# Seven-product second MoE: narrowing steps spread anew, second pass with 512 tokens first, products stored from ACT's queue

## The chip, the core and the metric

The kernel runs on one core of a Trainium2 chip. The metric is the device time of one execution in microseconds (us); three runs of the kernel before give its median.

## What is computed

A talking-heads attention over 1792 tokens feeds a first MoE layer (SoLU with a layer norm), which feeds a second one (squared ReLU). The result is the second layer's output, 1792 x 768, in float32.

```python
def _moe_ref(x, w_in, w_out, g_ln):          # d_model 768, d_ff 1024
    h = x @ w_in
    e = np.exp(h - np.max(h, axis=-1, keepdims=True))
    solu = h * (e / (np.sum(e, axis=-1, keepdims=True) + 1e-09))
    ...
    return (ln @ w_out).astype(np.float32)    # ln: solu normalised over d_ff, times g_ln

def _moe2_ref(x, w_in, w_out):                # d_model 768, d_ff 2048
    r = np.maximum(x @ w_in, 0.0)
    return (r * r @ w_out).astype(np.float32)

def reference(...):
    x = attention(q, k, v, w_pre, w_post)     # 1792 tokens x 768
    x = _moe_ref(x, **moe)
    return _moe2_ref(x, **moe2)
```

## The kernel before

**Split numbers.** TensorE multiplies in fp32r. Each float32 operand is split into a high part (a cast, on ACT) and a low part (a subtraction, on DVE or POOL), and each product is the sum of three matmuls.

**Three stages.** Attention takes the first 466 us and is not touched. The first MoE goes in tiles of 128 tokens, m = 0 to 13, until about 720 us. The second MoE takes the rest.

**First MoE, one tile.** PE computes `h1(m)`, 36 matmuls of 128 x 512. DVE then runs the norm, `norm1(m)`, from the maximum at L652 to the scaling at L668. PE transposes the previous tile (`zt`, L685; copied by ACT at L687 and DVE at L688). Every three tiles the output products `out1` become due, 24 matmuls each into a bank called ps_o; from m = 4 two of them run per tile, 20 in the loop. ACT copies each from ps_o into a tile o (L707, two buffers), and its DMA to x2D (L708) is issued by SP. Ten further products run behind the loop.

**Narrowing.** The second MoE's weights lie in memory as 64-bit floats. Beside the first MoE and the start of the second, 64 pieces of 128 x 384 are brought to float32. For each piece ACT computes a square wsq (L75, one buffer), and DVE runs four steps: L76, L80, L84 and L88; L88 needs wsq. Then SP stores the piece to w2D and loads the piece after next into the raw tile wr (two buffers). `filler()` is a call that runs one DVE step; the program places such calls by hand. In the loop there are 5 behind the norm of each tile from m = 4 and 4 behind each of its two `out1`, 13 per tile; the ten products behind the loop have three each. `need(n)` runs all steps that are missing when a load needs a piece.

**Second MoE.** d_ff is worked through in 8 steps of 256, twice: pass 0 for tokens 0 to 1023, pass 1 for tokens 1024 to 1791. `GRP` cuts each pass into two token groups, q = 0 and q = 1. A step is (it, q), it = 0 to 15. In a step PE first computes `h2` of the **next** step (L930, 36 matmuls of as many columns as the group has tokens), then `y2` of this step: seven products (a Strassen-like scheme), each of one to two blocks of three matmuls with 384 columns (L999), into one of three buffers ps_y. Each product is added to its own y on DVE (L1029). In it 0 there is nothing to add to, so y is a copy, from DVE (L1031) and ACT (L1033) by turns. The last it of each pass (7 and 15) is plain: seven sums on DVE (`join`, L992), then four products of twice the length and adds at L1017, each followed by a store.

Around it ACT computes relu and square (L938, L939) and the high parts of g, of the weights `ti` and `to` (L964, L834, L914). POOL computes the four sums s of the seven-product scheme (L953) and most low parts (L968, L838, L915). In the odd steps (q = 1) DVE computes two low parts of the next `ti` (L838), two of g (L968), four differences tT of the next `to` (L907, `sum_to`) and, in the second pass, two low parts of `to` (L915), all ahead of the step's adds; then come the narrowing steps. The tokens' tile x2 is loaded from x2D and split by `load_x2` and `split_x2` (L807 on ACT, L808).

**What sets the order.** The order on each engine is the order in which the program is written; engines wait for each other by semaphores. `hook(k)` is called behind product k and places the next step's splits of g there. Nothing reorders.

Of the kernel before, what the change touches and what calls it, by code (L numbers as in the profile page):

```python
# [18 lines left out]
def kernel(  # L19
# [16 lines left out]
    nc = tc.nc  # L36
    B, D, _ = qT.shape
# [8 lines left out]
    CC = DM // 128  # L46
# [7 lines left out]
    x2D = dram.tile([DM, NT], F32, name="x2D")  # L54
# [3 lines left out]
    NE = F2 // FE  # L58
# [67 lines left out]
    for b in range(B):  # L126
        for (i0, n) in CHUNKS:
            c, nb, oa = len(chunks), -(-n // R), 0
# [288 lines left out]
    def h1(m):  # L417
        t = xs.pop(m)
        pool = psi_p if m % 2 else psh_p
        ps = pool.tile([128, 2, 512], F32, tag="h", name="ps_h")  # L420
        for cc in range(CC):
            for (a, w) in ((0, 0), (0, 1), (1, 0)):
                for u in range(2):
                    nc.tensor.matmul(  # L424
                        out=ps[:, u],
                        lhsT=t[:, a, cc],
                        rhs=w1i[cc][:, w, u * 512:(u + 1) * 512],
                        start=(cc == 0 and a == 0 and w == 0),
                        stop=(cc == CC - 1 and a == 1),
                    )  # L430
            yield True
        hps[m] = ps

    def run(part):
        for _ in part:
            pass
# [184 lines left out]
    def load_w1_out(kk):  # L621
        r = m1_p.tile([128, DM], F32, tag="raw", name="w1oraw", bufs=3)
        nc.sync.dma_start(out=r, in_=w1oD[kk * 128:(kk + 1) * 128, :])
        return r
# [7 lines left out]
    def load_x(m):  # L632
        r = m1_p.tile([128, CC, 128], F32, tag="raw", name="xraw", bufs=3)
        nc.sync.dma_start(
            out=r, in_=xD[:, m * 128:(m + 1) * 128].rearrange("(c p) t -> p c t", p=128)
        )
        return r

    def split_x(m, r):
        t = m1_p.tile([128, 2, CC, 128], F32R, tag="xs", name="xs", bufs=2)  # L640
        nc.scalar.copy(t[:, 0], r)
        nc.gpsimd.tensor_tensor(out=t[:, 1], in0=r, in1=t[:, 0].bitcast(F32), op=ALU.subtract)
        xs[m] = t
# [48 lines left out]
    def out1(grp, cc):  # L692
        zT = zts[grp]
        t0 = grp * GT * 128
        width = min(GT * 128, NT - t0)
        ps = ps1_p.tile([128, 512], F32, tag="o", name="ps_o", bufs=2)
        for k in range(K1):
            for i, (w, a) in enumerate(((0, 0), (0, 1), (1, 0))):
                nc.tensor.matmul(  # L699
                    out=ps[:, 0:width],  # L700
                    lhsT=w1o[k][:, w, cc * 128:(cc + 1) * 128],
                    rhs=zT[:, a, k, 0:width],
                    start=(k == 0 and i == 0),
                    stop=(k == K1 - 1 and i == 2),
                )
        o = m1_p.tile([128, GT * 128], F32, tag="o", name="o1", bufs=2)
        nc.scalar.copy(o[:, 0:width], ps[:, 0:width])  # L707
        nc.sync.dma_start(out=x2D[cc * 128:(cc + 1) * 128, t0:t0 + width], in_=o[:, 0:width])  # L708

    w2raw = {}  # L710
    stored = [0]
# [34 lines left out]
    for m in range(NTILE):  # L746
        if m + 2 < NTILE:
            xr[m + 2] = load_x(m + 2)
        if m:
            run(h1(m))  # L750
        norm = norm1(m)
        next(norm)
        if m > 0:
            zt(m - 1)
        run(norm)
        if m + 2 < NTILE:
            split_x(m + 2, xr.pop(m + 2))
        for kk in range(len(w1o), min(K1, len(w1o) + 2)):
            wr[kk] = load_w1_out(kk)
        for kk in sorted(wr):  # L760
            split_w1_out(kk, wr.pop(kk))
        for _ in range(5 if m > GT else 0):
            filler()
        if m > GT and (m - 1) % GT == 0:
            outs += [((m - 1) // GT - 1, cc) for cc in range(CC)]
        for _ in range(2):
            if outs:
                out1(*outs.pop(0))
                for _ in range(4):
                    filler()  # L770


# [5 lines left out]
    wi2 = tc.tile_pool(name="wi2", bufs=1, side="left", reuse_waits="tile")  # L778
    wi2_p = wi2.__enter__()
    TG = 512  # L780
    GRP = [[(0, 512), (512, 512)], [(1024, 256), (1280, 512)]]
    NI = 2 * NE
    x2 = {}
    x2r = []
# [1 line left out]
    def load_x2(p, q, c):  # L786

        t0, n = GRP[p][q]
        k = TG // n
        r = wi2_p.tile([128, TG], F32, tag="x2r", name="x2r", bufs=3)  # L790
        nc.sync.dma_start(
            out=r.rearrange("p (k t) -> p k t", k=k),
            in_=x2D[c * 128:(c + k) * 128, t0:t0 + n].rearrange("(k p) t -> p k t", p=128),
        )
        x2r.append(r.rearrange("p (k t) -> p k t", k=k))

    def split_x2(p, q, c, eng):
        n = GRP[p][q][1]
        k = TG // n
        if c % 2 == 0:  # L800
            pool = wi2_p if q == 0 or c == 0 else m2_p
            t = pool.tile([128, 2, 2, TG], F32R, tag=f"x2_{q}_{c // 2}", name="x2")
            x2.setdefault((p, q), []).append(t)
        t = x2[p, q][-1]
        hi, lo = [t[:, a, c % 2:c % 2 + k, 0:n] for a in range(2)]
        r = x2r.pop(0)
        nc.scalar.copy(hi, r)  # L807
        eng.tensor_tensor(out=lo, in0=r, in1=hi.bitcast(F32), op=ALU.subtract)  # L808
# [101 lines left out]
    def split_to(it, k0, k1):  # L910
        for k in range(k0, min(k1, len(bsrc[it]))):
            r = bsrc[it][k]
            t = m2_p.tile([128, 2, HM], F32R, tag="to", name="to", bufs=9)
            nc.scalar.copy(t[:, 0], r)  # L914
            (nc.vector if it >= NE and k < 2 else nc.gpsimd).tensor_tensor(  # L915
                out=t[:, 1], in0=r, in1=t[:, 0].bitcast(F32), op=ALU.subtract
            )
            to.setdefault(it, []).append(t)
# [4 lines left out]
    def h2(it, q):  # L923
        n = GRP[it // NE][q][1]
        rs = []
# [32 lines left out]
    def hi_g(it, q):  # L958
        g = gs.setdefault((it, q), [])
        k = len(g)  # L960
        if k < len(gsrc[it, q]):
            w = GRP[it // NE][q][1] // 2
            g.append(m2_p.tile([128, 2, TG // 2], F32R, tag="g", name="g", bufs=9)[:, :, 0:w])
# [8 lines left out]
    def store_y(p, q, i, u, t):  # L972
        t0, n = GRP[p][q]
        w = n // 2
# [4 lines left out]
    def join(p, q):  # L979

        na = GRP[p][q][1] // 256
        p1, p2, p6, p7, p5, p4, p3 = [t[:, 0:na] for t in ys.pop((p, q))]
# [60 lines left out]
    for c in range(2, CC):  # L1043
        split_x2(0, 1, c, nc.vector)
        if c + 3 < CC:
            load_x2(0, 1, c + 3)
    sum_to(0)
    split_to(0, 0, 2)
    for j in range(4):
        load_ti(1, j)  # L1050
# [5 lines left out]
    for i, (it, q) in enumerate(steps):  # L1056
        p, e = divmod(it, NE)
        more = i + 1 < len(steps)
        nxt = it + 1 < NI

        if q and nxt:
            for j in (2, 3):
                ti_lo(it + 1, j, nc.vector)
        for k in range(2):
            lo_g(it, q, k, nc.vector)
        if q == 0:
            split_to(it, 2, 7)
            if nxt:
                for j in range(2):
                    ti_hi(it + 1, j)  # L1070
                    ti_lo(it + 1, j, nc.gpsimd)
        elif nxt:
            sum_to(it + 1)
            split_to(it + 1, 0, 2)
        if e == NE - 2 and q == 1:
            join(p, 0)
        if e == NE - 1 and q == 0:
            join(p, 1)
        if p == 0 and e == NE - 1:
            if q == 0:  # L1080
                for c in range(0, CC, 2):
                    split_x2(1, 0, c, nc.vector)
                    load_x2(1, 1, c // 2)
            else:
                for c in range(3):
                    split_x2(1, 1, c, nc.vector)
                    load_x2(1, 1, c + 3)
        for _ in range((5 if q else 11) + (4 if it == 0 else 0)):
            filler()
        if more:  # L1090
            h2(*steps[i + 1])

        if q == 0:
            if nxt:
                for j in (2, 3):
                    ti_hi(it + 1, j)
                load_to(it + 1, B[3])
        elif it + 2 < NI:
            for j in range(4):
                load_ti(it + 2, j)  # L1100
        if it == NE - 2 and q == 1:
            for c in range(0, CC, 2):
                load_x2(1, 0, c)

        def hook(k):
            if more:
                g = gs[steps[i + 1]]
                hi_g(*steps[i + 1])
                if len(g) > k + 2:
                    lo_g(*steps[i + 1], k + 2, nc.gpsimd)  # L1110
            if it == NE - 1 and q == 1 and k < 3:
                split_x2(1, 1, k + 3, nc.gpsimd)

        y2(it, q, hook)
        if q and it + 2 < NI:
            for fu in B[:3]:
                load_to(it + 2, fu)
# [58 lines left out]
```

## Time and profile before

| | us |
|---|---|
| median of three runs | 1237.52 |
| lowest and highest run | 1234.03, 1239.85 |
| the profiled execution | 1237.23 |
| its span in the trace | 1235.5 |
| PE busy | 1167.3 (94%) |
| DVE busy | 899.6 (73%) |
| ACT busy | 594.8 (48%) |
| POOL busy | 527.3 (43%) |
| first MoE's tiles with narrowing (DVE, L652 of m = 4 to L652 of m = 13) | 502.33 to 668.06 |

A timeline row holds the start, the time until the last of its instructions ended, the engine, the line, the operation, the tiles (written <- read), and how many instructions were put together; a bracket gives the idle time before it and what ended that. A matmul's end is modelled, and a busy PE may be slower than it could be, so the length of rows of like work is to be compared too.

### The profile page before, as it was taken

The numbers are of one execution on the slowest core, as the hardware profiler recorded it, in microseconds if no ns is written. First come the engines' busy times: TensorE is split into PE (matmuls) and PEld (weight loads), VectorE is DVE, ScalarE is ACT, GpSimd is POOL, SyncE is SP. The second block draws the span as 40 slices with busy tenths as digits, with TensorE's granted clock in tenths as the row PEclk, the third lists the DMA queues.
The fourth block names the chain that finished last, engine by engine and source line by source line (L and its number), as shares of the span: only waits on it lengthen the run. The fifth ranks groups of instructions, "written<-read, shape, count | busy, mean of one in ns | idle before, by whom it ended". The sixth has DMA issues, their size and how long they took to land. (4 is left out here: it accounts for less than half of the span.)

```text
span 1235.5 us, 22011 instructions
## 1 busy us (share of the span) xinstructions
PE 1167.3 (94%) x7599; PEld 975.5 (79%) x7599; DVE 899.6 (73%) x1612; ACT 594.8 (48%) x1485; POOL 527.3 (43%) x696
## 2 busy tenths in 40 slices
PE   9999999999999999999997995899999999999888
PEld 4777777777777778899986974788888898888777
DVE  4777777767776666777677567798888784777775
ACT  4565655666666544423322344643454446554441
POOL 2342233223222435311010356666657638777760
PEclk9999999999999999999999897999899999999999
DMA  6874765576574442544544763433342243212202
GB/s 175 214 208 161 215 196 182 184 212 194 159 218 144 147 147 91 156 126 143 166 131 121 239 201 92 145 128 110 102 129 64 77 148 110 71 58 62 65 10 77
DMA packets 131690, 172.19 MB, mean 139 GB/s; under 512 B 24443, under 2 KB 114171, under 8 KB 131579
## 3 DMA queue, kind: packets, MB, share of 16 engines
q1 hardware_dynamic: 130795, 170.51, 45.4%
q8 instruction: 61, 1.00, 0.3%
q14 instruction: 50, 0.41, 0.1%
q10 hardware_dynamic: 784, 0.27, 0.1%
HBM read 96.82 MB, written 35.39 MB: 107 GB/s over the span
## 5 line engine op out<-in xcount | busy, mean ns | idle before, releaser
L999 PE MATMUL ps_y<-to,g 128*128 128x384 f32 x1197 | 233.1, 352 | 45.3 <-DVE y L1029 26.9
L999 PEld LDWEIGHTS ps_y<-to,g 128*128 128x128 f32 x1197 | 221.3, 199 | 54.2 <-ACT r L938 24.6
L930 PE MATMUL ps_h<-x,ti 128*128 128x512 f32 (+1 forms) x1152 | 240.7, 366 | 1.7 <-ACT x L807 1.1
L930 PEld LDWEIGHTS ps_h<-x,ti 128*128 128x128 f32 x1152 | 197.7, 189 | 38.3 <-DVE x L808 2.0
L293 PEld LDWEIGHTS ps_post<-w,e 120*112 120x112 f32 (+1 forms) x1440 | 168.3, 177 | 67.5 <-issue 48.3
L307 DVE COPY at<-ps_post 112x480 f32<-112x480 f32 x180 | 117.1, 651 | 108.6 <-PE ps_post L293 108.1
L1029 DVE TENSOR_TENSOR y<-ps_y,y 128x768 f32<-128x768 f32 (+1 forms) x168 | 139.2, 854 | 65.3 <-PE ps_y L999 60.6
L293 PE MATMUL ps_post<-w,e 120*112 120x120 f32 (+1 forms) x1440 | 182.5, 270 | 2.0 <-ACT w L280 1.5
L256 ACT ACTIVATE e<-ps_pre,nm 120x448 f32<-120x448 f32 x180 | 114.6, 637 | 131.8 <-POOL w L273 73.3
L231 PE MATMUL ps_pre<-sdst,wpre_bd 120*120 120x448 f32 x360 | 166.3, 545 | 0.8 <-ACT e L256 0.7
L273 POOL TENSOR_TENSOR w<-wpost_bd,sm 120x120 f32<-120x120 f32 x166 | 64.0, 406 | 188.6 <-DVE sm L267 178.3
L75 ACT ACTIVATE wsq<-wr 128x384 f32<-128x384 f32 x64 | 35.6, 556 | 210.6 <-DVE wt L88 123.4
L699 PE MATMUL ps_o<-zt,w1o 128*128 128x384 f32 (+1 forms) x720 | 124.8, 334 | 11.3 <-ACT o L707 11.3
L699 PEld LDWEIGHTS ps_o<-zt,w1o 128*128 128x128 f32 x720 | 120.9, 196 | 12.5 <-ACT o L707 12.4
L424 PE MATMUL ps_h<-w1i,xs 128*128 128x512 f32 x504 | 119.3, 393 | 0.4 <-ACT xt L335 0.4
L244 DVE TENSOR_REDUCE nm<-ps_pre 120x1 f32<-120x448 f32 x180 | 110.1, 612 | 7.2 <-PE ps_pre L231 4.5
L424 PEld LDWEIGHTS ps_h<-w1i,xs 128*128 128x128 f32 x504 | 93.9, 188 | 20.0 <-ACT xt L335 0.6
L213 ACT COPY ssrc<-ps_qk 120x448 f32<-120x448 f32 (+1 forms) x186 | 84.9, 543 | 10.2 <-PE ps_qk L204 10.2
L953 POOL TENSOR_TENSOR s<-r 128x256 f32<-128x256 f32 (+1 forms) x56 | 42.0, 751 | 109.9 <-ACT r L939 109.9
L968 POOL TENSOR_TENSOR g<-s,g 128x256 fp32r<-128x256 f32 (+1 forms) x112 | 83.3, 764 | 6.1 <-ACT g L964 5.1
L938 ACT ACTIVATE r<-ps_h 128x512 f32<-128x512 f32 (+1 forms) x64 | 34.5, 539 | 105.1 <-PE ps_h L930 105.1
L320 PEld LDWEIGHTS ps_av<-at,v 112*64 112x64 f32 x1536 | 73.8, 137 | 12.2 <-ACT ssrc L213 5.3
(92 smaller groups left out, 1625.6 us busy)
## 6 DMA issues: line engine op xcount, KB each, us to landing
sdst<-ssrc SPq DMA_DIRECT2D x172, 210.0 KB
wr<-in_moe_w_in_dram SPq DMA_DIRECT2D x32, 384.0 KB
w2D<-wt SPq DMA_DIRECT2D x64, 192.0 KB
wr<-in_moe_w_out_dram SPq DMA_DIRECT2D x32, 384.0 KB
tir<-w2D SPq DMA_DIRECT2D x64, 192.0 KB
tor<-w2D SPq DMA_DIRECT2D x64, 192.0 KB
w1raw<-in_moe_w_in_dram SPq DMA_DIRECT2D x24, 256.0 KB
w1raw<-in_moe_w_out_dram SPq DMA_DIRECT2D x24, 256.0 KB
```

Of the source, the lines that this page charges most:

```text
L213: (nc.vector.tensor_copy if dve else nc.scalar.copy)(ssrc[c][0:n, h, :], ps[0:n, 0:S])
L231: nc.tensor.matmul(out=ps[0:m, 0:S], lhsT=wpre_bd[0:m].rearrange("p i g -> p (i g)")[:, 0:m], rhs=d[0:m], start=True, stop=True,)
L244: nc.vector.tensor_reduce(out=nm[0:m], in_=ps[0:m, 0:S], op=ALU.max, axis=AX.X, negate=True)
L256: nc.scalar.activation(out=e[0:m], in_=ps[0:m, 0:S], func=AF.Exp, bias=nm[0:m], scale=1.0, accum_out=sm[0:m])
L293: nc.tensor.matmul(out=ps[:, j, :, 0:r], lhsT=e[0:m, j * JW:(j + 1) * JW], rhs=w[0:m, :, 0:r], start=True, stop=True,)
L307: nc.vector.tensor_copy(at[c][:, :, :, oa:oa + r], ps[:, :, :, 0:r])
L424: nc.tensor.matmul(out=ps[:, u], lhsT=t[:, a, cc], rhs=w1i[cc][:, w, u * 512:(u + 1) * 512], start=(cc == 0 and a == 0 and w == 0), stop=( ...
L699: nc.tensor.matmul(out=ps[:, 0:width], lhsT=w1o[k][:, w, cc * 128:(cc + 1) * 128], rhs=zT[:, a, k, 0:width], start=(k == 0 and i == 0), st ...
L930: nc.tensor.matmul(out=ps[:, 0:n], lhsT=ti[it, f][:, w, cc], rhs=x2[it // NE, q][cc // 2][:, a, cc % 2, 0:n], start=(cc == 0 and i == 0), ...
L968: eng.tensor_tensor(out=t[:, 1], in0=gsrc[it, q][k], in1=t[:, 0].bitcast(F32), op=ALU.subtract)
L999: nc.tensor.matmul(out=ps[:, a, 0:HM], lhsT=g[:, ga, a * 128:(a + 1) * 128], rhs=t[:, wa], start=(f == 0 and j == 0), stop=(f == len(pairs ...
L1029: nc.vector.tensor_tensor(out=yo, in0=po, in1=yo, op=ALU.add)
```

## The change

Four things change.

- In the first MoE's loop each `out1` is followed by 5 narrowing steps, not 4: 15 per tile.
- In the second MoE the narrowing steps per step become 0 at (0,0), 9 at (0,1), then 6 at q = 0 and 8 at q = 1; they were 15, 9, 11 and 5. They end in it 5 or before in both kernels.
- In the second pass the groups are 512 tokens (q = 0) and 256 (q = 1); they were 256 and 512. With it go the loads and splits of x2 for this pass: its first group is loaded in three loads behind step (6,1) and split in step (7,0), three parts by DVE and three by POOL in the hooks; the second group is split by DVE in step (7,1). The two low parts of `to` for the last it move from DVE to POOL.
- The DMA that stores o to x2D is issued from ACT's queue.

```diff
@@ out1
-        nc.sync.dma_start(out=x2D[cc * 128:(cc + 1) * 128, t0:t0 + width], in_=o[:, 0:width])
+        nc.scalar.dma_start(out=x2D[cc * 128:(cc + 1) * 128, t0:t0 + width], in_=o[:, 0:width])
@@ first MoE's loop
                 out1(*outs.pop(0))
-                for _ in range(4):
+                for _ in range(5):
                     filler()
@@ second MoE
-    GRP = [[(0, 512), (512, 512)], [(1024, 256), (1280, 512)]]
+    GRP = [[(0, 512), (512, 512)], [(1024, 512), (1536, 256)]]
@@ split_to
-            (nc.vector if it >= NE and k < 2 else nc.gpsimd).tensor_tensor(
+            (nc.vector if NE <= it < NI - 1 and k < 2 else nc.gpsimd).tensor_tensor(
@@ the loop over steps
             if q == 0:
+                for c in range(3):
+                    split_x2(1, 0, c, nc.vector)
+                    load_x2(1, 0, c + 3)
+            else:
                 for c in range(0, CC, 2):
-                    split_x2(1, 0, c, nc.vector)
-                    load_x2(1, 1, c // 2)
-            else:
-                for c in range(3):
                     split_x2(1, 1, c, nc.vector)
-                    load_x2(1, 1, c + 3)
-        for _ in range((5 if q else 11) + (4 if it == 0 else 0)):
+        for _ in range((9 if it == 0 else 8) if q else (0 if it == 0 else 6)):
             filler()
...
         if it == NE - 2 and q == 1:
-            for c in range(0, CC, 2):
+            for c in range(3):
                 load_x2(1, 0, c)
...
-            if it == NE - 1 and q == 1 and k < 3:
-                split_x2(1, 1, k + 3, nc.gpsimd)
+            if it == NE - 1 and q == 0 and k < 3:
+                split_x2(1, 0, k + 3, nc.gpsimd)
+                load_x2(1, 1, 2 * k)
```

DVE in the first MoE's loop, from the end of tile 4's narrowing steps to those of tile 5 (wt, wr and wsq are narrowing's tiles, nm, sm and e the norm's); lines with + stand in the kernel after alone:

```order
 L88 SCALAR_TENSOR_TENSOR wt<-wsq,wt 128x384
 L76 TENSOR_SCALAR wt<-wr 128x384
+L80 SCALAR_TENSOR_TENSOR wt<-wr,wt 128x384
+L84 SCALAR_TENSOR_TENSOR wt<-wr,wt 128x384
 L652 TENSOR_REDUCE nm<-ps_h 128x1
 L656 TENSOR_SCALAR sm<-sm 128x1
```

Two more steps stand ahead of the next tile's norm, and the next tile begins in another place of a piece.

ACT at the start of the second MoE, in step (0,0): from the high parts of this step's `to` and the next step's `ti` to the relu of the next step's h (a number behind ps_h only tells one buffer from another). Before:

```order
L914 CAST to<-tT 128x384 x4
L914 CAST to<-tor 128x384
L834 CAST ti<-tir 128x384 x2
L75 ACTIVATE wsq<-wr 128x384 x4
L938 ACTIVATE r<-ps_h_8720 128x512
```

After:

```order
L914 CAST to<-tT 128x384 x4
L914 CAST to<-tor 128x384
L834 CAST ti<-tir 128x384 x2
L938 ACTIVATE r<-ps_h_8731 128x512
L939 ACTIVATE r<-r 128x512
```

The four squares of narrowing no longer stand between the splits and the relu.

DVE in the second pass, one it: the adds of q = 0, the odd step's own work, and the adds of q = 1. Before:

```order
L1029 TENSOR_TENSOR y<-ps_y,y 128x384 x7
L838 TENSOR_TENSOR ti<-tir,ti 128x384 x2
L968 TENSOR_TENSOR g<-r,g 128x256 x2
L907 TENSOR_TENSOR tT<-tor 128x384 x2
L907 TENSOR_TENSOR tT<-tor,tT 128x384
L907 TENSOR_TENSOR tT<-tT,tor 128x384
L915 TENSOR_TENSOR to<-tor,to 128x384 x2
L1029 TENSOR_TENSOR y<-ps_y,y 128x768 x7
```

After:

```order
L1029 TENSOR_TENSOR y<-ps_y,y 128x768 x7
L838 TENSOR_TENSOR ti<-tir,ti 128x384 x2
L968 TENSOR_TENSOR g<-r,g 128x128 x2
L907 TENSOR_TENSOR tT<-tor 128x384 x2
L907 TENSOR_TENSOR tT<-tor,tT 128x384
L907 TENSOR_TENSOR tT<-tT,tor 128x384
L915 TENSOR_TENSOR to<-tor,to 128x384 x2
L1029 TENSOR_TENSOR y<-ps_y,y 128x384 x7
```

The odd step's own work stands behind the wide adds now and in front of the narrow ones.

## Rows read from the trace of the kernel before

**Rows 1.** The page, part 1: engine, busy us (share of the span), instructions.

```profile
PE 1167.3 (94%) x7599; PEld 975.5 (79%) x7599; DVE 899.6 (73%) x1612; ACT 594.8 (48%) x1485; POOL 527.3 (43%) x696
```

**Rows 2.** Waits of PE: waiter <- releaser, us in total, times, longest.

```profile
PE ps_y L999 <- DVE y L1029: 26.9, 10, 4.9
...
PE ps_y L999 <- DVE y L1031: 15.3, 4, 13.2
...
PE ps_o L699 <- ACT o L707: 11.3, 3, 7.6
```

**Rows 3.** Timeline of PE, first MoE: start, length, engine, line, operation, count [idle before].

```profile
607.21 1.03 PE L685 MATMUL ps_tr<-id_sb,e 128*128 128x128 f32 x8
...
624.69 1.03 PE L685 MATMUL ps_tr<-id_sb,e 128*128 128x128 f32 x8
...
678.36 5.75 PE L699 MATMUL ps_o<-zt,w1o 128*128 128x384 f32 x24 [7.62 <-ACT o L707]
```

**Rows 4.** Timeline of DVE, first MoE, tile m = 4 and the last.

```profile
502.33 1.23 DVE L652 TENSOR_REDUCE nm<-ps_h 128x1 f32<-128x1024 f32 x1
...
509.13 2.19 DVE L668 TENSOR_SCALAR e<-e,mv,rs 128x1024 f32<-128x1024 f32 x1
...
512.89 0.56 DVE L88 SCALAR_TENSOR_TENSOR wt<-wsq,wt 128x384 f32<-128x384 f32 x1
...
517.90 0.36 DVE L76 TENSOR_SCALAR wt<-wr 128x384 uint32<-128x384 uint32 x1 [2.33 <-DMA wr<-in_moe_w_in_dram]
...
520.43 0.36 DVE L76 TENSOR_SCALAR wt<-wr 128x384 uint32<-128x384 uint32 x1 [0.31 <-DMA wr<-in_moe_w_in_dram]
520.71 1.22 DVE L652 TENSOR_REDUCE nm<-ps_h 128x1 f32<-128x1024 f32 x1
...
668.06 1.22 DVE L652 TENSOR_REDUCE nm<-ps_h 128x1 f32<-128x1024 f32 x1
```

**Rows 5.** Timeline of ACT, step (0,0).

```profile
756.35 0.58 ACT L938 ACTIVATE r<-ps_h 128x512 f32<-128x512 f32 x1
```

**Rows 6.** Timeline of POOL, step (0,0).

```profile
748.96 2.57 POOL L838 TENSOR_TENSOR ti<-tir,ti 128x384 fp32r<-128x384 f32 x2
758.89 0.73 POOL L953 TENSOR_TENSOR s<-r 128x256 f32<-128x256 f32 x1 [7.36 <-ACT r L939]
```

**Rows 7.** Timeline of PE, steps (0,0), (2,1) and (3,0).

```profile
758.47 2.26 PE L999 MATMUL ps_y<-to,g 128*128 128x384 f32 x6 [13.17 <-DVE y L1031]
760.91 4.42 PE L999 MATMUL ps_y<-to,g 128*128 128x384 f32 x18 [0.18 <-ACT y L1033]
...
836.25 8.32 PE L930 MATMUL ps_h<-x,ti 128*128 128x512 f32 x36
...
866.53 7.10 PE L999 MATMUL ps_y<-to,g 128*128 128x384 f32 x24 [3.16 <-DVE y L1029]
```

**Rows 8.** Timeline of DVE, a narrowing step in (2,0) and the adds of (2,1).

```profile
819.78 1.25 DVE L80 SCALAR_TENSOR_TENSOR wt<-wr,wt 128x384 uint32<-128x384 uint32 x1
...
845.67 7.21 DVE L1029 TENSOR_TENSOR y<-ps_y,y 128x768 f32<-128x768 f32 x7 [0.30 <-PE ps_y L999]
```

**Rows 9.** Timeline of PE, second pass, it 9 and 10.

```profile
1050.95 3.85 PE L999 MATMUL ps_y<-to,g 128*128 128x384 f32 x21
1054.64 4.46 PE L930 MATMUL ps_h<-x,ti 128*128 128x256 f32 x36
...
1064.68 4.43 PE L999 MATMUL ps_y<-to,g 128*128 128x384 f32 x24 [2.42 <-DVE y L1029]
...
1091.00 5.92 PE L999 MATMUL ps_y<-to,g 128*128 128x384 f32 x24 [2.42 <-DVE y L1029]
```

**Rows 10.** Timeline of DVE, second pass, step (9,1).

```profile
1055.31 1.63 DVE L838 TENSOR_TENSOR ti<-tir,ti 128x384 fp32r<-128x384 f32 x2
...
1063.59 6.51 DVE L1029 TENSOR_TENSOR y<-ps_y,y 128x768 f32<-128x768 f32 x7
```

**Rows 11.** Timeline of DVE, the last add.

```profile
1231.07 0.96 DVE L1017 TENSOR_TENSOR y<-ps_y,y 128x768 f32<-128x768 f32 x1 [1.13 <-PE ps_y L999]
```

## Prediction

> **What bounds the kernel now.** I read the busy times first: PE is busy 94% of the span [rows 1], so time is lost or won only where PE stands still, or where another engine makes it stand. The list of waits comes next: which releaser keeps PE from its next matmul [rows 2]. In the second MoE these are DVE's adds out of ps_y (L1029: ten waits, 26.9 us, the longest 4.9) and its copies (L1031: four, 15.3 us, one of 13.2); in the first MoE it is ACT's copy of o (L707: three, 11.3 us). Then I take each stretch by itself, because the share of the whole says nothing of them.
>
> In the first MoE PE's own tile takes 17.48 us, from one transpose group at 607.21 to the next at 624.69 [rows 3]. DVE's tile, from L652 to L652, takes (668.06 - 502.33) / 9 = 18.41 [rows 4]. DVE is the slower one, and the lag of 0.93 per tile gathers until it comes out as PE's wait of 7.62 at 678.36 [rows 3]: that copy L707 stands on ACT behind a wsq, and the wsq behind DVE's narrowing. So what DVE does per tile sets the end of this stretch.
>
> In the second MoE PE sets the pace (h2 of 512 tokens takes 8.3, [rows 7]), with holes: one of 13.17 in step (0,0), waits in the first pass's q=0 steps while narrowing runs, and one in each odd step of the second pass, 2.42 five times and 4.90 once [rows 2, 9].
>
> The profiled execution, 1237.23, agrees with the median 1237.52, so the sum goes against 1237.2.
>
> **A. First MoE: 15 narrowing steps a tile, not 13: +17.5.** L668 ends at 509.13 + 2.19 = 511.3, the piece behind it ends its L88 at 512.89 + 0.56 = 513.45: 2.13 us for four steps, 0.53 each. A piece's raw buffer is reloaded only after its L88, and the reload's data comes late: the third piece of the stretch starts at 517.90, 4.45 after the first's end, having waited 2.33; the fourth starts at 520.43, 4.85 after the second's end (513.45 + 2.13), waiting 0.31 [rows 4]. This 13-step stretch thus takes 520.71 - 511.3 = 9.4, and the rest of the tile 9.0. I run the same recurrence (2.13 a piece; the piece after next starts 4.45 to 4.85 behind an L88) for 15 steps, begun at the four places of a piece where tiles begin: 10.7, 12.5, 12.5 and 10.8. The mean is 11.64 where 13 steps give 9.6: +2.04 a tile. The two middle phases meet a fifth piece, that is a third load wait. Nine tiles lie between the L652 rows: two cycles of four and one short one give 103.8 against 86.4, +17.4, say +17.5. PE cannot hide it, being ahead of DVE already. Low end: the steps alone, 18 x 0.53 = +9.5. High end: one wait of 2.33 more on every second tile or so, 17.5 + 4 x 2.33, about +27. I take the recurrence, since its 13-step result reproduces 18.41 within 0.2 (9.0 + 9.6).
>
> The tenth tile's two added steps fall into the last ten products of this MoE, with three steps each as before. There they may cost PE up to +2. **The store of x2D from ACT's queue** acts in the same place: on SP it stood in front of narrowing's stores and loads, on ACT its issue stands before the next copy. In PE's waits for L707, 7.62 of 11.3 are DVE's lag [rows 2, 3]; so at most 3.7 can go. I set these two against each other at 0, ends +2 and -3.7.
>
> **B. Step (0,0): no narrowing: -9.** PE stops after three products and starts again at 758.47, when DVE's copy L1031 comes, behind 15 narrowing steps [rows 2, 7]; y2 ends with the 4.42 from 760.91, at 765.3. ACT's relu of the next h waits too, until 756.35, behind four wsq that wait for DVE [rows 5]. Without the steps DVE copies at once, and POOL is next: its splits end with the 2.57 from 748.96, at 751.5, and it then starts s of (0,1), which it does at 758.89 now [rows 6]. From that start to y2's end there are 6.4 now; with two products fewer left behind it, 4.5 to 5.5, so y2 ends at 756 to 757. That is -9; ends 0 and -13.2 (the hole). The stalls of (0,1) stay, since its nine steps stay.
>
> **C. First pass, it 1 to 4: -4.** The four L1029 waits here are 26.9 less the second pass's 5 x 2.42 + 4.90 = 17.0: 9.9. Behind three of them the 24 matmuls also run longer, up to 7.10 at 866.53 [rows 7] where 4.43 is normal [rows 9]; together 5.8. With 0.6 of another wait: 16.3 to be had, of which q=0's eleven steps are the cause. There they run beside POOL's splits, and cost 1.25 each (L80 at 819.78, [rows 8]) instead of 0.56; five fewer give back some 6 us a step, more than any of the waits. So all 16.3 go. But the q=1 steps get three more, 3 x 0.53, and one more load wait of about 2: +3.5. In step (2,1) DVE now waits 0.30 for PE's first product before its adds begin at 845.67 [rows 8]. PE runs two more products (2.2, by 24 matmuls in 4.43) before it needs a buffer, and an add of 768 takes 0.96 [rows 11], so DVE may come 1.2 + 0.3 later unseen: a new wait of 2.0 in four steps, 8, and by the pattern above some 4 of slower matmuls behind them. 12 - 16.3 = -4. Ends: -12 (no new load wait) and +4 (slower matmuls behind each).
>
> The Trainium skill ("SBUF — State Buffer", § Who interferes with whom) says that a DVE instruction with two SBUF inputs contends with a GpSimd instruction that reads SBUF. The 1.25 against 0.56 agrees; by the rule the added q=1 steps, if POOL runs there too, would take 1.25 each too, an estimate of 4 x 3 x 0.7 = +8 on C, which would then be +4 instead of -4 (it goes into C's high end, no further).
>
> **D. Second pass, 512 tokens first: -20.5.** Now, in an odd step, PE has ended y2(it,0) at 1050.95 + 3.85 = 1054.8, gives h2 of 256 tokens (4.46) and three products (18 matmuls, 3.3 by the 24 in 4.43; [rows 9]); DVE comes out of its odd-step work (sums and splits, from 1055.31) only at 1063.59 [rows 10], and PE waits 2.42. After the change PE has h2 of 512 (8.3) and three half-width products (1.7) in front: it needs the first buffer at E + 9.9, E being the end of y2(it,0). DVE's last add of 768 is 0.5 later than one of 384, so its odd work begins at E + 1.0, takes the same 8.3 and the first half-width add 0.5: the buffer is free at E + 9.8. Without the crowding by POOL it would be E + 6. So five waits of 2.42 go to about 0, and four rows of 24 matmuls return from 5.9 to 4.4 (5.92 against 4.43, [rows 9]), 6.0. Of the 4.90 I leave 1.5, of the rest 1. 17.0 + 6.0 = 23, less 2.5: -20.5. Even steps: h2 of 256 and seven products of 512, DVE idle before; nothing is late there. Ends: -23.5 and 0.
>
> The turn between the passes is moved about: three lower halves go from DVE to POOL a step earlier, and loads come a step later. PE has no wait there now, and DVE gets three subtractions fewer in front of its last adds; cost 0. Bound: POOL's three (1.29 each for 384 columns by the row at 748.96, [rows 6]; 1.7 for 512) all late, +5. split_to for the last step goes from DVE to POOL: part of the 4.90 above.
>
> **E. The end: -0.7.** The last y2 holds 256 tokens, so the last add, 0.96 from 1231.07 [rows 11], halves, and its store too; a slightly larger wait before it takes some back. Ends 0 and -1.5.
>
> Sum: 17.5 + 0 - 9 - 4 - 20.5 - 0.7 = -16.7: 1220.5, called 1220.
>
> **Rivals.**
> 1. The first MoE hides the two steps (A = 0), because loads are what DVE waits for and steps only fill waits. Against it: the wait is in front of the third piece, and steps behind it add to the tile whatever they replace. 1220 - 17.5 = 1203.
> 2. D gives nothing. In the odd step DVE's ten two-input operations run beside POOL's work for the wider h. If each waits for one POOL operation of 0.73 (758.89, [rows 6]), DVE's odd work ends at E + 12, PE waits 2.1 to 2.6 as before: 1220 + 20.5 = 1240, no change. For it: L838's two take 0.82 each there [rows 10], and narrowing's uncrowded L88 0.56 [rows 4]. Against: in today's even steps POOL has the same wide work, and its steps fit. The Trainium skill's section named above says that the shared port pair is an exclusive lock; by that rule this is the case, and the 0.82 so far bears out only part of it.
> 3. Slower: every 15-step stretch meets one more late load. The loads' delay grows as more of them are issued per tile. Each of the nine tiles then loses about 2.9 more, +26: 1246. It decides from 1.9 a tile. Against: the delay behind an L88 is 4.45 and 4.85, near equal, so the queue is not crowded.
> 4. The change doesn't do what it says in the second MoE: the moved steps make as large holes in the odd steps as those removed (C = +6) and (0,0) gains half. 1220 + 10 + 4.5 = 1235.
>
> **How the numbers follow.** Forecast 0.60 (its own range 1209 to 1231), rival 1 0.12, rival 2 0.13, rival 3 0.08, rival 4 0.07. Time: 1220. The range 1203 to 1240 takes in rival 4 and about half of rivals 1 and 2, and leaves out rival 3 and the tails. A measurement here tells 0.5% (6 us) from no change: below 1231.3 is faster, above 1243.7 slower. Faster: 0.59 + 0.12 + 0.02 = 0.73; same: 0.13 + 0.05 + 0.01 = 0.19; slower 0.08.
>
> **What would show it.** A: DVE's L652 to L652 in the first MoE at about 20.4 for tiles of 17.5 on PE, third load waits in half the tiles, and PE's waits on L707 at 25 to 30 in sum. B: the hole of 13.17 down to some 4, ended by ACT behind POOL's s. C: no wait at q=0 and new ones of about 2 at q=1 until narrowing ends. D: no L1029 wait from it 9 to 13. The forecast is wrong if the first MoE grows by under 10 or over 27, or if the waits of 2.4 are still in the second pass.

## The result

| | us |
|---|---|
| before, median of four runs on the same chip | 1238.5 |
| after, median of four runs | 1222.3 (1219.7 to 1224.6) |
| ratio | 0.9875, interval 0.984 to 0.991 |
| predicted | 1220, range 1203 to 1240 |
| profiled execution of after: span | 1222.9 (before: 1235.5) |

The kernel is 1.25% faster, and the forecast's time lies 2 us off. One term of its sum, C, had the wrong sign all the same. The account by stretches, from starts of h2 groups in the two traces of PE:

| stretch | before | after | difference | forecast |
|---|---|---|---|---|
| A. start to the second MoE's first h2 | 720.2 | 737.0 | +16.8 | +17.5 |
| B. from there to the end of step (0,0) | 45.0 | 35.7 | -9.3 | -9 |
| step (0,1) | 18.2 | 17.6 | -0.5 | 0 |
| C. steps (1,0) to (5,0) | 157.7 | 159.8 | +2.1 | -4 |
| D, E. step (5,1) to the end | 294.4 | 272.8 | -21.6 | -21.2 |
| sum | | | -12.6 | -16.7 |

The medians differ by 16.2 and the two traces by 12.6 only, since the profiled execution of after is the slowest of its four and that of before lies under its median. So by stretches the forecast is 4 off.

PE's waits in after (waiter <- releaser, total us, times, longest) stand against [rows 2]:

```profile
PE ps_o L699 <- ACT o L707: 18.0, 6, 7.0
...
PE ps_y L999 <- DVE y L1029: 16.5, 5, 3.8
...
PE ps_y L999 <- ACT y L1033: 5.7, 3, 4.2
...
PE ps_tr L685 <- DVE e L668: 3.6, 2, 2.4
```

The waits for the adds L1029 fell from 26.9 to 16.5, the hole behind L1031 is gone, and the first MoE's wait for L707 grew. Where the waits lie, PE's timeline of after shows (columns as in [rows 3]):

```profile
736.96 9.73 PE L930 MATMUL ps_h<-x,ti 128*128 128x512 f32 x42
...
770.54 2.29 PE L999 MATMUL ps_y<-to,g 128*128 128x384 f32 x6 [4.23 <-ACT y L1033]
772.63 9.89 PE L930 MATMUL ps_h<-x,ti 128*128 128x512 f32 x36
...
856.03 4.40 PE L999 MATMUL ps_y<-to,g 128*128 128x384 f32 x24 [3.52 <-DVE y L1029]
...
891.17 5.99 PE L999 MATMUL ps_y<-to,g 128*128 128x384 f32 x24 [3.79 <-DVE y L1029]
...
1082.69 7.45 PE L999 MATMUL ps_y<-to,g 128*128 128x384 f32 x42
1089.98 8.32 PE L930 MATMUL ps_h<-x,ti 128*128 128x512 f32 x36
1098.14 3.84 PE L999 MATMUL ps_y<-to,g 128*128 128x384 f32 x21
...
1196.44 4.18 PE L999 MATMUL ps_y<-to,g 128*128 128x384 f32 x12 [3.35 <-DVE y L1029]
```

The hole of 13.17 at (0,0) [rows 7] has become 4.23. In the first pass the waits have moved to q = 1 (3.52 is step (2,1), 3.79 step (3,1); two more of 2.21 and 3.68). In the second pass, where [rows 9] had 2.42 in every odd step, PE runs through, until (14,1) with 3.35.

### The profile page after: what moved, and what is told of

Same layout as the page of the kernel before. It is cut to its first block, busy times and chain, and to the rows that moved or that the text cites. A ratio compares the mean times of both kernels' runs of the same rounds, so it can differ in the third digit from the quotient of the medians.

```text
span 1222.9 us, 22004 instructions
## 1 busy us (share of the span) xinstructions
PE 1166.2 (95%) x7599; PEld 975.6 (80%) x7599; DVE 886.8 (73%) x1610; ACT 593.6 (49%) x1485; POOL 527.2 (43%) x698
## 5 line engine op out<-in xcount | busy, mean ns | idle before, releaser
L999 PE MATMUL ps_y<-to,g 128*128 128x384 f32 x1197 | 226.1, 345 | 23.9 <-DVE y L1029 16.5
L999 PEld LDWEIGHTS ps_y<-to,g 128*128 128x128 f32 x1197 | 215.7, 194 | 31.0 <-ACT r L938 14.4
L1029 DVE TENSOR_TENSOR y<-ps_y,y 128x768 f32<-128x768 f32 (+1 forms) x168 | 140.9, 855 | 50.6 <-PE ps_y L999 44.1
L699 PE MATMUL ps_o<-zt,w1o 128*128 128x384 f32 (+1 forms) x720 | 131.5, 345 | 18.0 <-ACT o L707 18.0
L75 ACT ACTIVATE wsq<-wr 128x384 f32<-128x384 f32 x64 | 35.7, 557 | 227.0 <-DVE wt L88 113.2
L699 PEld LDWEIGHTS ps_o<-zt,w1o 128*128 128x128 f32 x720 | 126.8, 204 | 20.2 <-ACT o L707 20.1
L953 POOL TENSOR_TENSOR s<-r 128x256 f32<-128x256 f32 (+1 forms) x56 | 38.6, 689 | 111.3 <-ACT r L939 111.3
L665 POOL TENSOR_TENSOR rs<-mv,eps_sb 128x1 f32<-128x1 f32 x14 | 2.7, 192 | 188.9 <-DVE mv L663 188.9
```

Of the source, the lines that this page charges most:

```text
L699: nc.tensor.matmul(out=ps[:, 0:width], lhsT=w1o[k][:, w, cc * 128:(cc + 1) * 128], rhs=zT[:, a, k, 0:width], start=(k == 0 and i == 0), st ...
L999: nc.tensor.matmul(out=ps[:, a, 0:HM], lhsT=g[:, ga, a * 128:(a + 1) * 128], rhs=t[:, wa], start=(f == 0 and j == 0), stop=(f == len(pairs ...
L1029: nc.vector.tensor_tensor(out=yo, in0=po, in1=yo, op=ALU.add)
```

## The experiments

Each edit is shown against the kernel after, unless it says otherwise. Line numbers of DVE's adds and of h2 move by one to six lines in kernels with added lines.

**The two halves of the change apart.** First the new groups without the new spread, then the new spread without the new groups.

```diff
@@ e1_groups_alone
-        nc.scalar.dma_start(out=x2D[...], in_=o[:, 0:width])
+        nc.sync.dma_start(out=x2D[...], in_=o[:, 0:width])
-                for _ in range(5):
+                for _ in range(4):
-        for _ in range((9 if it == 0 else 8) if q else (0 if it == 0 else 6)):
+        for _ in range((5 if q else 11) + (4 if it == 0 else 0)):
@@ e2_spread_alone (against the kernel before)
-                for _ in range(4):
+                for _ in range(5):
-        for _ in range((5 if q else 11) + (4 if it == 0 else 0)):
+        for _ in range((9 if it == 0 else 8) if q else (0 if it == 0 else 6)):
```

> Only the second pass's part of the change: 512 tokens first, with its loads and splits of x2 and the last step's two low parts on POOL. Narrowing is spread as before (13 steps a tile, 15/9 in it 0, 11/5 after), and x2D is stored from SP's queue. If the terms of the sum add up as the two traces read (second pass and end -21.6, rest 0 here), this takes 1216 to 1218: faster than the whole change, because narrowing's new spread costs more than it brings. If the new spread is needed for the second pass to keep its gain, it takes 1230 or more.

> Only the new spread of narrowing (15 steps a tile; 0/9, then 6/8), groups and store of x2D as before. Traces of the whole change: first MoE +16.75, step (0,0) -9.3, (0,1) -0.5, the first pass's steps 1 to 4 +2.1: 1238 + 9 = 1247, slower than before. By the forecast's terms (+17.5, -9, -4): 1243. If the new spread helps: under 1238.

Measured: 1215.4 (ratio 0.9805, interval 0.977 to 0.984) and 1245.3 (ratio 1.0061, 1.004 to 1.008), beside 1237.4 before. The groups alone (with their loads and splits) bring 22, the spread alone costs 8; the sum, -14, stands beside the -16 of the whole change. So the change is faster because of one part, and the other part takes a third of the gain away.

**The store of x2D.**

```diff
@@ e3_x2d_sync
-        nc.scalar.dma_start(out=x2D[...], in_=o[:, 0:width])
+        nc.sync.dma_start(out=x2D[...], in_=o[:, 0:width])
```

> The whole change but for the store of x2D, which SP issues as before. Theory: no difference, 1222 within 2 us, since a store of w2D follows its L88 at once in the loop. Rival: in the ten products behind the loop SP's queue holds the loads back behind the copies: PE's waits for L707 there (1.64 and 2.96 with the change) grow by 2 to 4, 1225.

Measured: 1222.7, ratio 0.9881 (0.985 to 0.991): no difference. The queue of this store doesn't matter.

**What the 15 steps wait for.** A third buffer for the raw tile lets the load of a piece go out one piece earlier. Room for it is taken from the first MoE's raw tokens and weights; the second kernel here takes that room alone, as a control.

```diff
@@ e4_raw3
-        raw = nar_p.tile([128, 384], I64, tag="wr", name="wr", bufs=2)
+        raw = nar_p.tile([128, 384], I64, tag="wr", name="wr", bufs=3)
         load_w2(1)
+        load_w2(2)
-            load_w2(i + 2)
+            load_w2(i + 3)
@@ e4_raw3 and e8_xraw2
-        r = m1_p.tile([128, DM], F32, tag="raw", name="w1oraw", bufs=3)
+        r = m1_p.tile([128, DM], F32, tag="raw", name="w1oraw", bufs=2)
-        r = m1_p.tile([128, CC, 128], F32, tag="raw", name="xraw", bufs=3)
+        r = m1_p.tile([128, CC, 128], F32, tag="raw", name="xraw", bufs=2)
```

> The whole change, and a third buffer for narrowing's raw tile, so that the load of a piece is issued one piece earlier (the first MoE's raw tokens and weights have two buffers instead of three, for room). If a tile of the first MoE is long because DVE waits for loads issued only after L88 (the recurrence), a 15-step stretch takes 15 x 0.53 = 8.0, DVE's tile 17.0, and PE's 17.5 sets the pace: the second MoE begins at about 713 instead of 737, and the new waits at q = 1 shrink from 3.3 to under 2 each: 1193 in all. If the loads are short of bandwidth, the waits stay: 1215 to 1222.

> The whole change, with two buffers instead of three for the first MoE's raw tokens and weights, and nothing else: what the third raw buffer of narrowing had to be paid with. In that run's trace the tiles m = 1 to 3 of the first MoE took 10.7 to 11.1 instead of 9.1 to 9.4; if that is the price of the two buffers, this takes 1227, and the third buffer of narrowing by itself brings some 32. If it costs nothing, 1222.

Measured: 1195.6 (ratio 0.9658) and 1231.0 (ratio 0.9950, 0.993 to 0.997). The room costs 9, more than the 5 expected, and the third buffer by itself brings 1231.0 - 1195.6 = 35, more than the whole change. DVE's waits for loads into wr are 57.0 in the control and gone with the third buffer. The second MoE begins 23.5 earlier than in the control; the other 12 come behind that. DVE's timeline of one tile with three buffers:

```profile
594.07 0.35 DVE L76 TENSOR_SCALAR wt<-wr 128x384 uint32<-128x384 uint32 x1
...
596.18 0.35 DVE L76 TENSOR_SCALAR wt<-wr 128x384 uint32<-128x384 uint32 x1
...
598.30 0.35 DVE L76 TENSOR_SCALAR wt<-wr 128x384 uint32<-128x384 uint32 x1
...
601.63 0.36 DVE L76 TENSOR_SCALAR wt<-wr 128x384 uint32<-128x384 uint32 x1 [1.13 <-DMA w2D<-wt]
```

Three pieces follow each other at 2.1. The wait that is left is for the store of an earlier piece out of wt, which has two buffers; such waits are 21.7 in sum, and most of the later tiles take 17.9 to 19.0 on DVE, not the 17.0 that I expected. The second MoE began at 722.8, not 713 (9 of it for the room).

**13 steps when loads come early.**

```diff
@@ e5_raw3_13 (e4_raw3, and)
-                for _ in range(5):
+                for _ in range(4):
-        for _ in range((9 if it == 0 else 8) if q else (0 if it == 0 else 6)):
+        for _ in range((5 if q else 11) + (4 if it == 0 else 0)):
```

> The third raw buffer and the new groups, with narrowing spread as before the change (13 steps a tile, 15/9, 11/5) and x2D stored from SP's queue. If the order of steps matters only through load waits, 13 steps leave DVE's tile at 15.9 to 17, under PE's 17.5: the second MoE begins at 712, some 10 before the run with 15 steps and three buffers, but the hole of 13 in step (0,0) is back (9 worse), and q = 0 has waits of 1 to 3 again: 1195, equal to that run. If 15 steps are the better place once loads come early: 1200 or more.

The kernel that ran differs from this text in one point: it stores x2D from ACT's queue, as the kernel after does. By e3_x2d_sync that makes no difference.

Measured: 1197.1, ratio 0.9687 (0.966 to 0.971), equal to the run with 15. PE's timeline of it shows both sides of the trade, the second MoE's begin at 710.5 (12 before the run with 15) and the hole:

```profile
710.52 9.73 PE L931 MATMUL ps_h<-x,ti 128*128 128x512 f32 x42
...
746.85 2.26 PE L1000 MATMUL ps_y<-to,g 128*128 128x384 f32 x6 [11.23 <-DVE y L1032]
```

**The first pass's steps.**

```diff
@@ e9_steps_11_5
-        for _ in range((9 if it == 0 else 8) if q else (0 if it == 0 else 6)):
+        for _ in range((9 if it == 0 else 5) if q else (0 if it == 0 else 11)):
```

> The whole change, but from it 1 on the narrowing steps stand as before: 11 at q = 0 and 5 at q = 1 (instead of 6 and 8). By the forecast's term C the new 6 and 8 bring 4, so this takes 1226. By the two traces, in which that stretch takes 157.7 and 159.8, they cost 2, so this takes 1220, with waits of 1.3 to 3.2 at q = 0 and none at q = 1.

Measured: 1221.4, ratio 0.9872 (0.985 to 0.990). The time can't be told from the change's own, and 1226 is excluded. So 6 and 8 bring nothing against 11 and 5. In the trace the stretch of C takes 155.5, less than the 159.8 of the change, and its waits stand at q = 0 again, this time mostly behind ACT, whose splits of ti stand behind a square of narrowing:

```profile
839.53 4.43 PE L999 MATMUL ps_y<-to,g 128*128 128x384 f32 x24 [3.33 <-ACT ti L834]
```

**The sums at the end of the second pass.** `join` of the first group (seven sums of 768 columns) is cut: five sums in (14,1), two in (15,0). In another kernel the two low parts of the last `to` go back to DVE.

```diff
@@ e12_join5
         if e == NE - 2 and q == 1:
-            join(p, 0)
+            joining = join(p, 0)          # yields behind each sum
+            for _ in range(5 if p else 8):
+                next(joining, None)
         if e == NE - 1 and q == 0:
-            join(p, 1)
+            run(joining)
+            run(join(p, 1))
@@ e6_split_dve
-            (nc.vector if NE <= it < NI - 1 and k < 2 else nc.gpsimd).tensor_tensor(
+            (nc.vector if it >= NE and k < 2 else nc.gpsimd).tensor_tensor(
```

> The whole change, and only the seven sums of the second pass's first group cut into five in (14,1) and two in (15,0). The trace of the change has 3.35 of wait behind the seven, and DVE has some 2.6 to spare in the odd steps before. If the wait is the sums' length (9.1 us beside POOL), five sums end 2.6 earlier and the wait shrinks to about 0.7: 1219.5. If it only moves to (15,0): 1222.

> The whole change, but the two low parts of the last step's weights `to` stay on DVE, behind the sums. By the forecast they are part of the wait at (14,1): 2 x 0.6 to 0.8 later adds, 1223.5. If POOL's copy of them delays POOL's own work there as much, 1222.

Measured: 1216.7, ratio 0.9823 (0.980 to 0.984), and 1221.4, ratio 0.9860 (0.984 to 0.988). The cut sums give some 5, of which the trace accounts for about 4 at (14,1): DVE's sums take 9.13 in the kernel after,

```profile
1186.70 9.13 DVE L992 TENSOR_TENSOR y<-y 128x768 f32<-128x768 f32 x7
```

and in the kernel with five of them

```profile
1183.39 6.87 DVE L992 TENSOR_TENSOR y<-y 128x768 f32<-128x768 f32 x5
```

while PE's wait there falls from 3.35 to 1.08, and the matmuls behind it from 4.18 to 2.33:

```profile
1190.87 2.33 PE L1000 MATMUL ps_y<-to,g 128*128 128x384 f32 x12 [1.08 <-DVE y L1030]
```

The two low parts are worth nothing on either engine.

**All together.** With three raw buffers, DVE waited for stores out of wt; with the second MoE begun earlier, the steps' distribution and the sums were left.

```diff
@@ e10_all (e4_raw3's third buffer, and)
-            t = nar_p.tile([128, 384], F32, tag="wt", name="wt", bufs=2)
+            t = nar_p.tile([128, 384], F32, tag="wt", name="wt", bufs=3)
-        r = m1_p.tile([128, DM], F32, tag="raw", name="w1oraw", bufs=3)
+        r = m1_p.tile([128, 384], F32, tag="o", name="w1oraw", bufs=3)    # loaded and split in halves
-        o = m1_p.tile([128, GT * 128], F32, tag="o", name="o1", bufs=2)
+        o = m1_p.tile([128, GT * 128], F32, tag="o", name="o1", bufs=3)
-        r = m1_p.tile([128, CC, 128], F32, tag="raw", name="xraw", bufs=3)
+        r = m1_p.tile([128, CC, 128], F32, tag="raw", name="xraw", bufs=1)
-        for _ in range((9 if it == 0 else 8) if q else (0 if it == 0 else 6)):
+        for _ in range((9 if it == 0 else 7) if q else (0 if it == 0 else 7)):
-        if e == NE - 2 and q == 1:
-            join(p, 0)
+        if it == NE - 2 and q == 1:
+            join(0, 0)
+        if it == NI - 1 and q == 0:
+            join(1, 0)
```

In e10_all all seven sums of the second pass's first group thus stand in (15,0). The next kernel, e11_all_8_6, has 8 steps at q = 0 and 6 at q = 1 in place of 7 and 7, and the sums cut as in e12_join5; e13_all_7_7 has the cut sums with 7 and 7.

> The whole change and what the runs so far point to: three raw buffers and three buffers of the finished piece wt (DVE waited 21.7 us for stores of wt with two), room for them by loading the first MoE's weights in halves into o's buffers (three of them) with one buffer for raw tokens; 7 and 7 steps at q = 0 and q = 1 from it 1 on; and the seven sums of the second pass's first group one step later, in (15,0), where 3.4 of wait stood at (14,1). First MoE at PE's own 17.5 a tile, so that the second MoE begins at about 707; waits in its first pass under 1 each: 1175 to 1180. If DVE then waits for loads again (bandwidth), 1190.

> As the run with everything (three raw buffers, three of wt, halves in o's buffers), with two differences: 8 and 6 narrowing steps at q = 0 and q = 1 from it 1 on (7 and 7 left waits of 0.3 to 1.8 at q = 1), and of the seven sums of the second pass's first group five in (14,1), two in (15,0) (all seven in (15,0) left a wait of 3.5 there). Both waits gone: 1184 - 3.5 - 3 = 1178. If the steps' crowding at q = 0 or the other sums bring new waits, 1184 stays.

> Everything that helped: three raw buffers, three of wt, halves in o's buffers, 7 and 7 steps at q = 0 and q = 1 from it 1 on, and five of the seven sums in (14,1), two in (15,0). Against the run with all seven sums in (15,0), where 3.5 of wait stood, about 1.1 is left at (14,1): 1184.3 - 2.4 = 1182. If 8 and 6 steps were not what made the run with them slower, but the sums, this takes 1186 again.

Measured: 1184.3 (ratio 0.9573), 1186.8 (0.9586) and 1181.5 (0.9537, interval 0.950 to 0.958). The first two miss what was expected of them, the third meets it. In the first the second MoE begins at 712.4, not 707, and PE waits once in (15,0) for the sums that were moved there:

```profile
1169.60 3.60 PE L1004 MATMUL ps_y<-to,g 128*128 128x384 f32 x14 [3.48 <-DVE y L1022]
```

The second has no wait there, but more of those in the first pass (waits list of the run with 8 and 6):

```profile
PE ps_y L1005 <- DVE y L1035: 9.1, 7, 1.8
```

against 7 and 7 with the cut sums:

```profile
PE ps_y L1005 <- DVE y L1035: 4.6, 5, 1.8
```

These two kernels differ in nothing else, and their times (1186.4 to 1189.3 and 1180.4 to 1182.4) don't overlap. So it was the 8 and 6 that made the second run no better. The last kernel still pays for the room of its buffers, for tile 4 of the first MoE begins at 508.5 instead of 501.5, but it is the best of this study, 4.6% under the kernel before; its PE is busy 98% of the span (part 1 of its page):

```profile
PE 1150.8 (98%) x7599; PEld 962.3 (82%) x7599; DVE 883.7 (75%) x1610; ACT 595.0 (50%) x1493; POOL 529.5 (45%) x706
```

## Why the prediction was right, point by point

**A held, and for its reason.** Nine tiles took 182.8 on DVE (L652 at 501.46 and 684.29) against 165.7: +17.1, where the recurrence gave +17.4. It also gave the shape: the four tiles of nine in which a fifth piece is met took 20.4 to 22.4 (mean 21.6, forecast 21.5) and have a third load wait, of 0.3 to 3.0; the other five took 18.2 to 19.8. Here is such a tile of after, from L652 to L652, 22.4, with three load waits:

```profile
541.30 1.22 DVE L652 TENSOR_REDUCE nm<-ps_h 128x1 f32<-128x1024 f32 x1
...
555.56 0.36 DVE L76 TENSOR_SCALAR wt<-wr 128x384 uint32<-128x384 uint32 x1 [2.10 <-DMA wr<-in_moe_w_in_dram]
...
558.35 0.36 DVE L76 TENSOR_SCALAR wt<-wr 128x384 uint32<-128x384 uint32 x1 [0.58 <-DMA wr<-in_moe_w_in_dram]
...
563.44 0.36 DVE L76 TENSOR_SCALAR wt<-wr 128x384 uint32<-128x384 uint32 x1 [2.89 <-DMA wr<-in_moe_w_in_dram]
563.72 1.22 DVE L652 TENSOR_REDUCE nm<-ps_h 128x1 f32<-128x1024 f32 x1
```

The third wait is for a single step's sake: L76 of the fifth piece waits 2.89, and so from the L88 before it (its end is at 560.56) to L652 that one step costs 3.2. Rivals 1 and 3 fall with this. The runs with a third raw buffer show what the load waits were worth: nine tiles of 15 steps take 185.5 in the control and 167.8 with it. The two steps are not free there either: with 13 steps (e5_raw3_13) nine tiles take 158.1, 9.7 less, while DVE waits for stores of wt in both. Only with a third wt as well (e13_all_7_7) do 15 steps take 159.7. So the price was paid in waits for buffers, first for the load's and then for the store's. The prediction's check on L707 (25 to 30 in sum) was wrong, 18.0, because another 3.6 of PE's lag stood in two waits of the transposes for DVE's L668, and a part in matmuls that ran longer: from the first of these L652 to the second MoE's begin PE was busy for 213.8 instead of 206.6 with the same matmuls, at a granted clock of 0.94 instead of 0.97. The zero for the tenth tile and the store of x2D held; the store alone was measured at no difference.

**B held.** The wait of 13.17 became 4.23, ended by ACT behind POOL's sums, as described; y2(0,0) ended 35.7 after the first h2 began instead of 45.0. ACT's timeline of after shows the sum that it waits for and the copy that frees PE's buffer at 770.5:

```profile
768.39 0.41 ACT L964 CAST g<-s 128x256 fp32r<-128x256 f32 x1 [4.49 <-POOL s L953]
...
769.70 0.79 ACT L1033 COPY y<-ps_y 128x768 f32<-128x768 f32 x1
```

**C failed.** It was to bring 4 and cost 2.1. The q = 0 waits went, as said. The new waits at q = 1 were 2.21, 3.52, 3.79 and 3.68 instead of 2.0 each, and the matmuls behind them cost 5.5 instead of 4. The failed step is the +3.5, by which DVE comes later in an odd step: it counts three more steps and a load wait and takes the odd step's other work as fixed. On DVE that work (L838 to L907, eight operations) comes first, then the narrowing steps, then the adds that free PE's buffers. In step (2,1) of after:

```profile
842.12 1.88 DVE L838 TENSOR_TENSOR ti<-tir,ti 128x384 fp32r<-128x384 f32 x2
...
854.66 0.36 DVE L76 TENSOR_SCALAR wt<-wr 128x384 uint32<-128x384 uint32 x1 [1.44 <-DMA wr<-in_moe_w_out_dram]
854.94 6.50 DVE L1029 TENSOR_TENSOR y<-ps_y,y 128x768 f32<-128x768 f32 x7
```

From L838 to the adds 12.8 pass here, and 8.0 did before. In all four steps what exceeds 9.3 is PE's wait, so the "1.2 + 0.3 later unseen" was nearly right, 1.3. Busy times of each engine in stretches that hold exactly the eight operations, step (2,1) before:

```profile
837.30:842.80 5.50, 5.50 (x26) 4.56 (x25) 5.41 (x10) 0.00 (x0) 2.34 (x3) 1.00 0.01 3
```

and after, steps (2,1) and (3,1):

```profile
842.10:849.50 7.40, 7.40 (x35) 6.16 (x34) 7.31 (x10) 0.56 (x2) 5.81 (x6) 1.00 0.01 2
877.00:884.30 7.30, 7.30 (x34) 6.06 (x34) 7.21 (x10) 0.48 (x2) 5.72 (x6) 1.00 0.00 0
```

The columns are the stretch, its length, then the busy time and count of PE, its weight loads, DVE, ACT and POOL, then the clock as a share of full speed, the DMA share and GB/s. The same eight operations take 7.3 instead of 5.4, and POOL is busy beside them for 5.8 instead of 2.3. The length follows POOL within one kernel too. In e6_split_dve, where the narrowing behind takes 5.7 in both steps, they took 7.3 in (2,1) with 5.8 of POOL, and 5.4 in (3,1) with 2.2. PE's waits differ by the same 2:

```profile
856.79 6.89 PE L999 MATMUL ps_y<-to,g 128*128 128x384 f32 x24 [3.69 <-DVE y L1029]
...
892.35 4.40 PE L999 MATMUL ps_y<-to,g 128*128 128x384 f32 x24 [1.72 <-DVE y L1029]
```

What puts POOL there is argued from the traces. Before, PE's wait at q = 0 held DVE's adds back until POOL was nearly done; without that wait DVE can meet POOL, and I counted its removal as all gain. The wait alone doesn't decide: in step (1,1) the eight operations took 6.6 before, behind a wait of 1.30, and 5.4 after, with none in front. There POOL's first sum began 1.9 after the end of h2 instead of 5.0, since ACT's relu no longer stood behind a square that waits for DVE (4.4 of it before). No run took POOL's work out of the odd step alone. Over the four steps DVE came 4.6 later on average where the prediction has 3.5: 3.2 by the narrowing steps and their load wait, as counted, and 1.35 by the eight operations.

The added steps cost what I said: the narrowing behind that work takes 5.5 to 6.1 in after, a load wait of 1.4 to 2.1 in it, and 2.6 before; its steps run at 0.56, not at the 1.25 that the prediction weighed. With the third buffer that load wait is gone, the narrowing takes 4.0, and the waits in (1,1) to (4,1) are none, 1.18, 1.86 and 1.03. So about half of C's new waits, 7.0 of 13.2, were the load waits, the rest steps and crowding.

The Trainium skill's section "Who interferes with whom" of the page "SBUF — State Buffer" says that such pairs of instructions contend; the two stretches agree with that. That section also calls the shared port pair an exclusive lock, so that one instruction would stand until the other has ended; the two stretches don't show this in full, for 3.5 us more of POOL beside DVE cost 1.9.

**D held, in its total partly by luck.** In the second pass the odd step's ten operations were to take "the same 8.3". They take 6.3, since POOL now has the narrow group's work there. First before (one stretch), then after (step (10,1), then step (8,1), where POOL stands still):

```profile
1055.30:1063.60 8.30, 6.96 (x50) 6.63 (x48) 8.21 (x12) 4.47 (x14) 8.22 (x11) 1.00 0.26 71
```

```profile
1091.10:1097.40 6.30, 6.30 (x29) 5.23 (x28) 6.17 (x11) 3.36 (x9) 4.26 (x7) 1.00 0.47 130
1041.80:1046.20 4.40, 4.40 (x21) 3.66 (x20) 4.28 (x11) 1.83 (x4) 0.00 (x0) 1.00 0.45 134
```

Counted as in the prediction, the first buffer is free some 2 before PE needs it, not 0.1; no L1029 wait is left from it 9 to 13. Rival 2 named the right mechanism and the wrong side: the crowding shrank. At (14,1) I left 1.5; 3.35 came, and the 12 matmuls behind it ran 2 longer. The seven sums are twice as wide in that step now and stand beside POOL (9.13 for seven); the cut sums confirm it. Another gain made up for this: its 9 to 13 took 116.5 instead of 136.1, which is 3.0 more than their five waits (12.1) and the slower rows behind three of them (4.5) had cost. No term of the prediction holds these 0.6 per it. The rows of h2 are a little shorter (8.32 instead of 8.50 for 512 tokens, 4.34 instead of 4.46 for 256); why stays open. Together with E: -21.6 against -21.2.

**The verdict** was right because A, B and D, each priced from rows of its own stretch, were within 1 us. That the total came so near is luck in part: C missed by 6, which the medians show less than the traces do, and inside D two misses cancelled. Rival 4 was right on C's sign (+2.1, not its +6) and wrong on (0,0). That the spread as a whole costs something was in the sum (17.5 - 9 - 4 = +4.5; measured 8), though I did not say that undoing it would be faster.

## To carry to other kernels

Before moving steps about, ask what each step waits for. Here one more buffer, so that a load goes out a piece earlier, brought 35 against its control, and the new spread, with 20 steps moved into the first MoE's loop, cost 8. A stage that is bound by another engine's order pays for each added step in full, plus the load wait that the step runs into. And a change of waits shifts engines against each other: price the next stretch with the neighbours that it will have, not with those that it had.

## What the runs showed of the hardware

- DVE's operations slow down with POOL beside them by degrees. Ten operations of the odd step took 4.4 with POOL idle, 6.3 with 4.3 of POOL in the stretch, and 8.3 with 8.2 (the last with two of them 256 columns wide instead of 128).
- Behind many of PE's waits of over 2 us the matmuls ran at a lower clock, with granted clocks of 0.58 to 0.73, and so took 1.5 to 2.7 longer (1.5 behind a wait of 4.90, 2.7 behind one of 3.16). The row of 24 matmuls in 7.10 [rows 7] lies in this stretch of before, whose granted clock is 0.58 of full speed, a mix of the two levels 1.2 and 2.4 GHz:

```profile
866.50:873.50 7.00, 6.97 (x25) 7.00 (x26) 4.41 (x5) 4.39 (x12) 6.48 (x10) 0.58 0.05 18
```

  In other rows no such cost follows (3.52 of wait at 856.03, then 24 matmuls in 4.40 at a clock of 1.00). What tells the two apart stays open. With most of the waits gone the mean clock rose from 0.976 to 0.993 in the best kernel.
